# GpSimd takes three of the first expert's weight subtractions, and the routing table's products are spread, in an attention and mixture-of-experts kernel

## The chip, the cores and the metric

The kernel runs on one core of a Trainium2 chip. Its time is the device time of one launch in microseconds, the median of the runs shown; three runs of the kernel before gave 868.94, 869.82 and 870.97 us. A core has five engines with a queue of instructions each: TensorE (PE, matrix products), VectorE (DVE), ScalarE (ACT), GpSimd (POOL) and SyncE (SP, which here issues DMAs). An instruction that needs another engine's result waits at the head of its queue, and all behind it on that engine wait too.

## The reference

Three layers in a row, all in float32:

```python
# 1. clustered attention: 2 batches, 8 heads, 768 rows, 64 columns
mask = q_assign[:, :, :, None] == k_assign[:, :, None, :]        # nearest of 16 centroids
scores = np.where(mask, scale * (q @ k.transpose(0, 1, 3, 2)), -1e9)
x = softmax(scores) @ v                                          # -> 1536 rows of 512

# 2. mixture of 8 experts, the two best of each row (D = 512, F = 1024)
noisy = x @ w_gate + np.log1p(np.exp(x @ w_noise)) * noise
top2_w = softmax over the two largest of noisy
out[mask] += top2_w[mask, k, None] * (np.maximum(x[mask] @ w1[e], 0.0) @ w2[e])

# 3. a second mixture of 8 experts: the best of each row, 384 rows per expert at most
out[i] = gate_w[i] * y[expert_idx[i], pos[i]]
```

The change lies in layer 2, in the passage from attention to the experts.

## The kernel before

**Products in float32.** A float32 operand is split into a high part of a shorter format and a low part, the rest. A product is the sum of three: high by high, high by low, low by high. The names end in `h` and `l`: `xh`, `xl` for rows of x, `wh`, `wl` for weights, `hh`, `hl` for the hidden layer. Splitting a weight takes two instructions per group of 1024 columns: ScalarE copies the raw weights into `wh` (L199), and VectorE subtracts, `wl = raw - wh` (L200). A weight matrix has four such groups; SP fetches them through four `raw` buffers (L187). Matrix n = 0 is the first expert's first weights, n = 1 its second, n = 2 the second expert's first.

**Jobs.** Expert 0's rows are done in two jobs of 256 rows, one per half of the batch: `jobs[0]` (rows of batch 0, known early) and `jobs[1]` (batch 1). Both use n = 0 and 1. A wide job goes over eight blocks f of 128 hidden columns (`wide1`, L1072: 12 products, then `hh` on ScalarE at L1074 and `hl` on VectorE at L1075), and then over tiles of 128 rows (`second`, L1117 to L1119: three products for each f, 24 for a tile), whose sum ScalarE copies to y (L1138) and GpSimd scatters to memory (L1159). For the next job GpSimd gathers rows (`xg`, L1010), TensorE turns them (`tp`, L1051), ScalarE makes `xh` (L1053) and VectorE `xl` (L1054).

**The route of the second half.** Beside `jobs[0]` runs `route1(1)`: which two experts each row of batch 1 goes to and at which place of their lists. It is a generator of small VectorE operations; at its end twelve pairs of one-hots (`one_hot`, L298 `ohp` and L300 `ohv`, four buffers each) are multiplied on TensorE and added up (L422) to a table of 96 columns; the sum (L424) and three more steps give `t1k` (L314), the row numbers by which `jobs[1]` gathers. Then come the counts `cnt1i`, which every engine reads into registers (L1440), and the gates (L444 to L470, stored at L472).

**What sets the order.** The order is written out by the program at build time with a planner's clock. `tick(us, pace)` is called between steps of TensorE's work; it hands us times pace units to the generators that run beside, and each `yield c` costs c units, a plain `yield` 1, and a negative c costs -c microseconds, whatever the pace (L962 to L975). The same `tick` lets at most one split of weights (`wstep`) be put into the order if the planner holds its data for landed (L957). `K0` to `K3` are costs inside `route1`. `wneed0(1)` puts one split of n = 1 into the order; `wneed(1)` all that are left. `settle` (L977) ticks until all generators are done.

The fetches of n = 2 wait for the rows: while `st["rush"]` is set none is issued, `gathers` (L1020) clears it, and the first fetch behind it gets a dependency on the last gather (L188).

Of the kernel before, what the change touches and what calls it, by code (L numbers as in the profile page):

```python
# [8 lines left out]
F32 = mybir.dt.float32  # L9
# [4 lines left out]
OP = mybir.AluOpType  # L14
# [12 lines left out]
def kernel(  # L27
# [17 lines left out]
    nc = tc.nc  # L45
# [19 lines left out]
    NJ1 = E + 2  # L65
    GT = 3
    F0, FP, T0, PA = 1, (2, 4), 1.5, 3.0
    K0, K1, K2, K3 = 10, 3, 1.5, 2
    NY = 4
    V0, V1, V2, V3 = 3, 4, 5, 3  # L70
    L1, L2 = 1, 2
# [104 lines left out]
    def wload(n):  # L176

        src = halves[n].rearrange("p (g c) f -> p g c f", g=4)
        nch = 4 * src.shape[2]
        k = 2 * E + 2 * NSP - 1  # L180
        buf = n % 3 if n < k else 3 if n == k else (n - 1) % 3
        for g in range(4):
            raw = {}

            def fetch(g=g, raw=raw):
                raw[0] = stage.tile([128, 1024], F32, name="raw")
                ins = nc.sync.dma_start(raw[0].rearrange("p (c f) -> p c f", c=nch // 4), src[:, g])  # L187
                if st.get("behind"):  # L188
                    tc.add_manual_dep(ins.ins, st.pop("behind").ins.name, mybir.DependencyInfo(
                        mybir.DependencyClass.Sync, mybir.DependencyReason.DATA), reason="the rows go first")  # L190
                clock["dma"] = max(clock["now"] + 2.0, clock["dma"]) + 1.46
                raw["at"] = clock["dma"] + 0.3
            chunks.append(fetch)
            cs = slice(g * 1024, (g + 1) * 1024)

            def op(cs=cs, raw=raw, g=g):
                wh, wl = WB[buf]
                W[n] = [w.rearrange("p (c f) -> p c f", c=nch) for w in (wh, wl)]
                nc.scalar.activation(wh[:, cs], raw[0], AF.Copy)  # L199
                nc.vector.tensor_tensor(wl[:, cs], raw[0], wh[:, cs].bitcast(F32), op=OP.subtract)  # L200
                clock["out"] -= 1
                wfill()

            def part(half, cs=cs, raw=raw, g=g):
                wh, wl = WB[buf]
                W[n] = [w.rearrange("p (c f) -> p c f", c=nch) for w in (wh, wl)]
                src = raw[0][:, half * 512:(half + 1) * 512]
                o = slice(cs.start + half * 512, cs.start + (half + 1) * 512)
                nc.scalar.activation(wh[:, o], src, AF.Copy)
                nc.gpsimd.tensor_tensor(wl[:, o], src, wh[:, o].bitcast(F32), op=OP.subtract)  # L210
                if half:
                    clock["out"] -= 1
                    wfill()
            if n:
                wops.append((n, raw, op))
            else:
                wops.extend((n, raw, lambda half=half, part=part: part(half)) for half in range(2))

    def wfill():
        while clock["out"] < st.get("ahead", SB) and chunks and not st.get("rush"):  # L220
            clock["out"] += 1
            chunks.pop(0)()
# [114 lines left out]
    def route1(b, psum):  # L337
# [61 lines left out]
        f = yield from split_slots(s2[:, 0:2].rearrange("p a j -> p (a j)"), 2 * J, "sf")  # L399

        if b == 0:
            st["cnt0"] = rt.tile([128, E], F32, name="cnt0")
            nc.vector.tensor_copy(st["cnt0"], tot)
            st["base"] = rt.tile([128, E], F32, name="base")
            nc.vector.tensor_add(st["base"], eoff1, tot)
            nc.vector.memset(st["base"][:, 0:1], float(S))
            nc.vector.memset(st["base"][:, E - 1:], float((E - 1) * T + S))
            yield
            at = rt.tile([128, 2 * J], I32, name="at0")
            nc.vector.scalar_tensor_tensor(at, f[:, 0], float(NC1), f[:, 1], op0=OP.mult, op1=OP.add)  # L410
            yield
            ptasks.append(place0(b, at))
        else:
            ps2 = psum()
            hots = []
            for j in range(J + 1):
                if j < J:
                    hots += [one_hot(f, c * J + j, code1[:, b, j, c:c + 1], NC1) for c in range(2)]
                    yield K2
                for c in range(2 if j else 0):  # L420
                    n = 2 * (j - 1) + c
                    nc.tensor.matmul(ps2[:, :NC1], *hots[n], start=(n == 0), stop=(n == 2 * J - 1))  # L422
            yield K3
            nc.vector.tensor_add(st["tab0"], ps2[:, :NC1], st["tab0"])  # L424
            yield
            st["dst1"], st["tok1"] = yield from finish_table(st["tab0"], "t1", True)
            cnt = rt.tile([128, 2 * NJ1], F32, name="cnt1")
            nc.vector.tensor_copy(cnt[:, 0:1], st["cnt0"][:, 0:1])
            nc.vector.tensor_copy(cnt[:, 1:2], tot[:, 0:1])
            nc.vector.tensor_add(cnt[:, 2:E], tot[:, 1:E - 1], st["cnt0"][:, 1:E - 1])  # L430
            nc.vector.tensor_copy(cnt[:, E:E + 1], st["cnt0"][:, E - 1:])
            nc.vector.tensor_copy(cnt[:, E + 1:NJ1], tot[:, E - 1:])
            yield
            nc.vector.tensor_sub(cnt[:, NJ1:], cnt[:, 0:NJ1], lim1)
            ci = rt.tile([128, NJ1 + 1], I32, name="cnt1i")
            nc.vector.tensor_copy(ci[:, 0:NJ1], cnt[:, 0:NJ1])
            yield
            over = rt.tile([128, 1], F32, name="over1")
            nc.vector.tensor_reduce(over, cnt[:, NJ1:], axis=AX.X, op=OP.max)
            yield  # L440
            nc.vector.tensor_scalar(ci[:, NJ1:], over, 0.0, None, op0=OP.max)
            st["cnt1f"], st["cnt1i"] = cnt, ci
            yield
# [495 lines left out]
    def wneed0(n=0):  # L939
        if wops and wops[0][0] <= n:  # L940
            wstep()
# [304 lines left out]
    def work(job, nxt, hook=None):  # L1246
# [32 lines left out]
        if job.wide:  # L1279
            for f in range(F0 if job is jobs[0] else 0, FC):  # L1280
                job.wide1(f, hh, hl)
                if job is jobs[0] and f % 2 == 0:
                    wneed0(1)
                tick(12 * job.n / 2400, PA if job is jobs[0] else 3.0)
        else:
            rest = job.tile1(0, hh, hl, tick, fill)
# [71 lines left out]
    def pool(ph, name, side="left"):  # L1358
# [5 lines left out]
    jobs = [Job(h=0, loads=([2], [], []), n=N2, col=0, key="tok0", src=x_dram[0:S], tok="tok0", dst="dst0", **dict(com, kind="first")),  # L1364
            Job(h=0, loads=([], [3], []), n=N2, col=R1 // 2, **late)]
# [158 lines left out]

    st["rush"] = True
    spawn(route1(1, mpsum))
    jobs[0].gathered = True
    tick(T0)
# [127 lines left out]
    for n, job in enumerate(every):  # L1656
        work(job, every[n + 1] if n + 1 < len(every) else None, hooks.get(n))
# [35 lines left out]
```

## Time and profile before

| | us |
|---|---|
| median of three runs | 869.82 (868.94 to 870.97) |
| the profiled execution, its own time | 877.53 |
| its span, first to last instruction | 875.8 |
| mean granted TensorE clock | 0.975 of full speed |
| PE busy | 838.8 (96%) |
| DVE busy | 541.9 (62%) |
| ACT busy | 498.1 (57%) |
| POOL busy | 280.9 (32%) |

The profile is of one execution. A time in it is from the start of the span. `x4` behind a row means that several instructions in a row are put together; square brackets give the idle time of the engine ahead of it and what ended it. Attention ends at about 291 us, `jobs[0]` goes on to 323, `jobs[1]` begins at 325. A granted clock of 1.00 is 2.4 GHz of TensorE, 0.50 is 1.2 GHz.

### The profile page before, as it was taken

To read this page: it belongs to the slowest core of one execution; us is meant where nothing else is said; L and a number is where in the kernel's file an instruction comes from. 1 tells how busy PE (TensorE), PEld (TensorE's weight loads), DVE (VectorE), ACT (ScalarE), POOL (GpSimd) and SP (SyncE) were. 2 spreads that over 40 slices of the span, in tenths; PEclk is the share of its full clock that TensorE was granted. 3 is DMA by queue.
4 is the path that set the end of the run, shared out by engine and by line. 5 is a ranking of instruction groups with operands and counts; after the bars stand their busy time and mean duration, and the time that the engine had idled before them with its cause. 6 is when DMAs were issued, how large, how long until landed. Compare 5 with 4: busy or idle time off the path is not lost. (4 is left out here: it accounts for less than half of the span.)

```text
span 875.8 us, 14860 instructions
## 1 busy us (share of the span) xinstructions
PE 838.8 (96%) x5371; PEld 748.1 (85%) x5371; DVE 541.9 (62%) x1110; ACT 498.1 (57%) x967; POOL 280.9 (32%) x465
## 2 busy tenths in 40 slices
PE   8899999999998989999999999999998988999997
PEld 6799999889987878989989898988987767888886
DVE  6888888989888656447444353535477337655270
ACT  5798988888998315445333343535344336555361
POOL 3445556447864021321302122033221112222110
PEclk9799999999999979999999999999899989999999
DMA  4005422411113035744644444458374318866250
GB/s 98 28 28 199 143 96 73 139 32 47 55 37 107 19 126 169 222 153 138 189 162 138 135 145 137 120 186 287 107 257 140 128 51 295 264 204 221 73 171 17
DMA packets 62189, 116.84 MB, mean 133 GB/s; under 512 B 13737, under 2 KB 25769, under 8 KB 62096
## 3 DMA queue, kind: packets, MB, share of 16 engines
q1 hardware_dynamic: 52832, 92.60, 33.1%
q0 software_dynamic: 9264, 23.06, 8.2%
q8 instruction: 51, 0.84, 0.4%
q14 instruction: 42, 0.34, 0.1%
HBM read 97.29 MB, written 23.74 MB: 138 GB/s over the span
## 5 line engine op out<-in xcount | busy, mean ns | idle before, releaser
L200 DVE TENSOR_TENSOR wl<-raw,wh 128x1024 fp32r<-128x1024 f32 x124 | 150.5, 1222 | 40.0 <-ACT wh L199 36.1
L1072 PE MATMUL l<-xh,wh 128*128 128x256 f32 (+1 forms) x508 | 156.4, 310 | 2.7 <-ACT xh L1053 1.2
L1072 PE MATMUL l<-xh,wl 128*128 128x256 f32 (+1 forms) x508 | 155.2, 308 | 0.2 <-DVE wl L200 0.2
L1072 PE MATMUL l<-xl,wh 128*128 128x256 f32 (+1 forms) x508 | 148.1, 307 | 0.0
L1117 PE MATMUL l<-wh,hh 128*128 128x512 f32 x328 | 137.1, 418 | 1.2 <-PEq L1445 0.4
L199 ACT ACTIVATE wh<-raw 128x1024 fp32r<-128x1024 f32 x124 | 128.9, 1053 | 4.9 <-DMA raw<-in_moe_w_dram 4.8
L1119 PE MATMUL l<-wh,hl 128*128 128x512 f32 x328 | 131.0, 399 | 0.0
L1118 PE MATMUL l<-wl,hh 128*128 128x512 f32 x328 | 130.4, 398 | 0.0
L1075 DVE SCALAR_TENSOR_TENSOR hl<-l,hh 128x256 fp32r<-128x256 f32 (+1 forms) x127 | 61.3, 484 | 98.4 <-ACT hh L1074 95.0
L1074 ACT ACTIVATE hh<-l 128x256 fp32r<-128x256 f32 (+1 forms) x127 | 55.1, 434 | 104.5 <-PE l L1072 102.9
L776 DVE TENSOR_TENSOR El<-et,Eh 128x384 fp32r<-128x384 f32 x192 | 101.2, 557 | 12.2 <-ACT Eh L775 10.0
L1072 PEld LDWEIGHTS l<-xh,wh 128*128 128x128 f32 x508 | 96.3, 190 | 6.2 <-issue 2.8
L744 DVE TENSOR_REDUCE nm<-st 128x1 f32<-128x768 f32 x96 | 91.4, 952 | 13.7 <-PE st L739 12.8
L1072 PEld LDWEIGHTS l<-xh,wl 128*128 128x128 f32 x508 | 96.1, 189 | 1.2 <-DVE wl L200 0.4
L775 ACT ACTIVATE Eh<-et 128x384 fp32r<-128x384 f32 x192 | 87.7, 495 | 12.5 <-PE et L770 12.2
L1072 PEld LDWEIGHTS l<-xl,wh 128*128 128x128 f32 x508 | 93.6, 188 | 0.2
L753 ACT ACTIVATE E<-st,nm 128x768 f32<-128x768 f32 x96 | 87.0, 907 | 8.2 <-DVE nm L744 7.9
L1159 POOL DMA_INDIRECT y_dram<-y,t1d x23 | 23.3, 1012 | 194.0 <-ACT y L1138 164.8
L770 PE MATMUL et<-identr,Er 128*128 128x128 f32 x576 | 72.6, 244 | 4.4 <-DVE El L776 2.4
L1119 PEld LDWEIGHTS l<-wh,hl 128*128 128x128 f32 x328 | 62.8, 191 | 15.0 <-DVE hl L1089 0.3
L770 PEld LDWEIGHTS et<-identr,Er 128*128 128x128 f32 x576 | 65.5, 142 | 11.0 <-DVE El L776 3.7
L1117 PEld LDWEIGHTS l<-wh,hh 128*128 128x128 f32 x328 | 62.8, 191 | 13.5 <-issue 1.5
(322 smaller groups left out, 1558.5 us busy)
## 6 DMA issues: line engine op xcount, KB each, us to landing
raw<-in_moe_w_dram SPq DMA_DIRECT2D x128, 512.0 KB, 4.5
vraw<-in_v_dram SPq DMA_DIRECT2D x16, 192.0 KB, 2.5
x_dram<-xp SPq DMA_DIRECT2D x8, 384.0 KB, 3.3
out_dram<-xg SPq DMA_DIRECT2D x1, 3072.0 KB, 10.2
y_dram<-xg SPq DMA_DIRECT2D x1, 3072.0 KB, 10.3
part<-y_dram SPq DMA_DIRECT2D x12, 256.0 KB, 3.7
yt<-y_dram SPq DMA_DIRECT2D x12, 256.0 KB, 3.9
x_dram<-part POOLq DMA_DIRECT2D x12, 256.0 KB, 3.7
```

The costliest lines, as they stand in the source:

```text
L199: nc.scalar.activation(wh[:, cs], raw[0], AF.Copy)
L200: nc.vector.tensor_tensor(wl[:, cs], raw[0], wh[:, cs].bitcast(F32), op=OP.subtract)
L744: nc.vector.tensor_reduce(nm, ps, axis=AX.XY, op=OP.max, negate=True)
L753: made = nc.scalar.activation(E, st.pop(("S", i, j))[:, :, :HW], AF.Exp, bias=st.pop(("nm", i, j)), accum_out=st["Z", i][:, j:j + 1])
L770: ins = nc.tensor.transpose(ps[:, n * 128:(n + 1) * 128].bitcast(F32R), E[:, part, n * 128:(n + 1) * 128], identr)
L775: nc.scalar.activation(Eh[o], ps, AF.Copy)
L776: nc.vector.tensor_sub(El[o], ps, Eh[o].bitcast(F32))
L1072: nc.tensor.matmul(ps[:, :n], (w1l if k == 2 else w1h)[:, c, fs], (self.xl if k == 1 else self.xh)[:, c, :n], start=(m == 0), stop=(m == l ...
L1075: nc.vector.scalar_tensor_tensor(hl[:, f, :n], ps[:, :n], 0.0, hh[:, f, :n].bitcast(F32), op0=OP.max, op1=OP.subtract)
L1117: nc.tensor.matmul(ps[:rows], hh[:, f, cs], w2h[:, f, :], start=(f == 0), stop=False)
L1118: nc.tensor.matmul(ps[:rows], hh[:, f, cs], w2l[:, f, :], start=False, stop=False)
L1119: nc.tensor.matmul(ps[:rows], hl[:, f, cs], w2h[:, f, :], start=False, stop=(f == FC - 1))
```

## The change

Three edits. The low parts of groups 1 to 3 of n = 1 are made on GpSimd in two halves of 512 columns instead of on VectorE in one piece. The four splits of n = 1 stand behind the blocks f = 2, 3, 4 and 6 (before: 2, 4 and 6, and the fourth behind f = 7). And the costs in `route1(1)` are others: K1 is 1 instead of 3; the first pair step costs 1 unit and each later one 0.88 us of the planner's clock, instead of 1.5 units each.

```diff
-    K0, K1, K2, K3 = 10, 3, 1.5, 2
+    K0, K1, K2, K3 = 10, 1, -0.88, 2
...
                 nc.scalar.activation(wh[:, cs], raw[0], AF.Copy)
-                nc.vector.tensor_tensor(wl[:, cs], raw[0], wh[:, cs].bitcast(F32), op=OP.subtract)
+                if n == 1 and g:
+                    for o in range(0, 1024, 512):
+                        at = slice(cs.start + o, cs.start + o + 512)
+                        nc.gpsimd.tensor_tensor(wl[:, at], raw[0][:, o:o + 512], wh[:, at].bitcast(F32), op=OP.subtract)
+                else:
+                    nc.vector.tensor_tensor(wl[:, cs], raw[0], wh[:, cs].bitcast(F32), op=OP.subtract)
                 clock["out"] -= 1
...
                     hots += [one_hot(f, c * J + j, code1[:, b, j, c:c + 1], NC1) for c in range(2)]
-                    yield K2
+                    yield K2 if j else 1
...
-                if job is jobs[0] and f % 2 == 0:
+                if job is jobs[0] and f in (2, 3, 4, 6):
                     wneed0(1)
```

Lines below the new code are numbered 5 higher in the changed kernel. On TensorE the twelve table products stood six behind the sixth group of the first tile and six behind its end; now they stand four behind the sixth group, two behind the tile's end, and two and four behind the second and fourth group of the second tile. On GpSimd six subtractions stand ahead of the scatter of the first tile. Further on the instructions are the same in the same order.

VectorE in the last blocks of `jobs[0]` before, up to the copy of the ranks (`l_4895` is the block f = 4, `l_4949` f = 7):

```order
L1075 SCALAR_TENSOR_TENSOR hl<-l_4895,hh 128x256
L200 TENSOR_TENSOR wl_4796<-raw,wh_4795 128x1024
L265 TENSOR_REDUCE fwm<-fw 128x6
L267 TENSOR_TENSOR oh_4848<-fw,fwm 128x48
L370 TENSOR_TENSOR A_4915<-oh_4848 128x48
L1075 SCALAR_TENSOR_TENSOR hl<-l_4917,hh 128x256
L1075 SCALAR_TENSOR_TENSOR hl<-l_4932,hh 128x256
L200 TENSOR_TENSOR wl_4796<-raw,wh_4795 128x1024
L1075 SCALAR_TENSOR_TENSOR hl<-l_4949,hh 128x256
L200 TENSOR_TENSOR wl_4796<-raw,wh_4795 128x1024
L379 COPY rs<-rps 128x56
```

The same place in the changed kernel (`l_4898` is f = 4, `l_4954` f = 7):

```order
L1080 SCALAR_TENSOR_TENSOR hl<-l_4898,hh 128x256
L270 TENSOR_REDUCE fwm<-fw 128x6
L272 TENSOR_TENSOR oh_4848<-fw,fwm 128x48
L375 TENSOR_TENSOR A_4919<-oh_4848 128x48
L1080 SCALAR_TENSOR_TENSOR hl<-l_4921,hh 128x256
L1080 SCALAR_TENSOR_TENSOR hl<-l_4936,hh 128x256
L1080 SCALAR_TENSOR_TENSOR hl<-l_4954,hh 128x256
L384 COPY rs<-rps 128x56
```

Three subtractions are gone from between the hidden layer's and the route's operations.

ScalarE at the end of `jobs[0]` before, from the copy of the first tile's sum to the first `hh` of `jobs[1]` (`wh_4797` is the matrix n = 2):

```order
L1138 ACTIVATE y<-l_4979 128x512
L447 ACTIVATE gt<-gt 128x6
L1053 ACTIVATE xh<-tp 128x4x128
L1138 ACTIVATE y<-l_5089 128x512
L1053 ACTIVATE xh<-tp 128x4x128
L1440 TENSOR_LOAD cnt1i
L1074 ACTIVATE hh<-l_5316 128x256
```

The same place in the changed kernel:

```order
L1143 ACTIVATE y<-l_4984 128x512
L452 ACTIVATE gt<-gt 128x6
L1143 ACTIVATE y<-l_5077 128x512
L199 ACTIVATE wh_4797<-raw 128x1024
L1445 TENSOR_LOAD cnt1i
L1058 ACTIVATE xh<-tp 128x4x128 x2
L1079 ACTIVATE hh<-l_5321 128x256
```

A copy of the matrix n = 2 and the register load stand ahead of both `xh`, which stood ahead of them.

VectorE at the same time before, from the gates to the first `hl` of `jobs[1]`:

```order
L461 TENSOR_TENSOR gates_105<-gw 128x6
L465 TENSOR_SCALAR gt<-s_5000 128x6
L466 TENSOR_SCALAR gt<-s_5000 128x6
L468 TENSOR_TENSOR gt<-gt 128x6
L470 TENSOR_TENSOR gates_105<-gates_105,gt 128x6x2
L1054 TENSOR_TENSOR xl<-tp,xh 128x4x128 x2
L1440 TENSOR_LOAD cnt1i
L1075 SCALAR_TENSOR_TENSOR hl<-l_5316,hh 128x256
```

And in the changed kernel:

```order
L466 TENSOR_TENSOR gates_105<-gw 128x6
L205 TENSOR_TENSOR wl_4798<-raw,wh_4797 128x1024
L463 TENSOR_TENSOR gw<-gt 128x6
L464 TENSOR_TENSOR gw<-gt,s_4997 128x6
L466 TENSOR_TENSOR gates_105<-gw 128x6
L470 TENSOR_SCALAR gt<-s_4997 128x6
L471 TENSOR_SCALAR gt<-s_4997 128x6
L473 TENSOR_TENSOR gt<-gt 128x6
L475 TENSOR_TENSOR gates_105<-gates_105,gt 128x6x2
L1445 TENSOR_LOAD cnt1i
L1059 TENSOR_TENSOR xl<-tp,xh 128x4x128 x2
L1080 SCALAR_TENSOR_TENSOR hl<-l_5321,hh 128x256
```

A subtraction for n = 2 stands in the middle of the gates, and the register load ahead of `xl`. On SP the four fetches of n = 2 stand ahead of the store of the gates, which stood ahead of them.

## Rows read from the trace of the kernel before

**Rows 1.** TensorE: line L1119 (ns, starts), then timeline (start, us, what, [idle]).

```profile
L1119 PE MATMUL l<-wh,hl x6: 389/396/397, 303.8 to 307.3; 128*128 128x512 f32 x6
...
308.77 2.53 PE L422 MATMUL rps<-ohv,ohp 128*128 128x96 f32 x6 [1.05 <-DVE ohv L300]
...
323.13 1.03 PE L1051 MATMUL tp<-ident,xg 128*128 128x128 f32 x8
325.39 0.38 PE L1072 MATMUL l<-xh,wh 128*128 128x256 f32 x1 [1.23 <-ACT xh L1053]
...
326.44 0.63 PE L1072 MATMUL l<-xl,wh 128*128 128x256 f32 x4
```

**Rows 2.** Windows: length, busy PE, PEld, DVE, ACT, POOL, clock, DMA share, GB/s.

```profile
307.70:311.10 3.40, 2.04 (x7) 1.38 (x7) 3.33 (x17) 0.00 (x0) 0.00 (x0) 0.80 0.00 0
311.10:319.80 8.70, 8.70 (x24) 6.87 (x25) 5.94 (x39) 0.80 (x2) 3.10 (x3) 0.50 0.19 59
```

**Rows 3.** VectorE's timeline, 304 to 326.

```profile
304.59 0.42 DVE L1075 SCALAR_TENSOR_TENSOR hl<-l,hh 128x256 fp32r<-128x256 f32 x1
304.92 1.21 DVE L200 TENSOR_TENSOR wl<-raw,wh 128x1024 fp32r<-128x1024 f32 x1
306.06 0.21 DVE L379 COPY rs<-rps 128x56 f32<-128x56 f32 x1
...
308.10 0.29 DVE L298 TENSOR_SCALAR ohp<-lane,sf 128x128 fp32r<-128x128 bf16 x1
...
308.54 0.28 DVE L298 TENSOR_SCALAR ohp<-lane,sf 128x128 fp32r<-128x128 bf16 x1
...
315.61 0.26 DVE L424 TENSOR_TENSOR tab<-rps,tab 128x96 f32<-128x96 f32 x1 [0.54 <-PE rps L422]
...
316.44 0.21 DVE L314 TENSOR_SCALAR t1k<-t1d 128x96 int32<-128x96 int32 x1
...
318.89 0.16 DVE L458 TENSOR_TENSOR gw<-gt 128x6 f32<-128x6 f32 x1
...
319.71 0.17 DVE L470 TENSOR_TENSOR gates<-gates,gt 128x12 f32<-128x12 f32 x1
...
325.37 0.69 DVE L1054 TENSOR_TENSOR xl<-tp,xh 128x512 fp32r<-128x512 f32 x1 [0.28 <-ACT xh L1053]
```

**Rows 4.** ScalarE's timeline, two rows.

```profile
303.16 0.38 ACT L1074 ACTIVATE hh<-l 128x256 fp32r<-128x256 f32 x1
...
324.74 0.60 ACT L1053 ACTIVATE xh<-tp 128x512 fp32r<-128x512 f32 x1
```

**Rows 5.** GpSimd, L210, the halves of n = 0: ns min/median/max, first and last start.

```profile
L210 POOL TENSOR_TENSOR wl<-raw,wh x8: 1269/1285/1299, 252.0 to 276.7; 128x512 fp32r<-128x512 f32 x8
```

**Rows 6.** Second gather, fetch behind it, SP's waits (us, times, longest), a landing.

```profile
318.25 1.00 POOL L1010 DMA_INDIRECT xg<-x_dram,t1k  x1 [0.30 <-issue]
...
321.67 1.77 SPq L187 DMA_DIRECT2D raw<-in_moe_w_dram  x4
...
SPq L187 <- DVE hl L1075: 10.4, 4, 5.1
SPq L187 <- DMA xg<-x_dram,t1k: 1.4, 1, 1.4
...
raw<-in_moe_w_dram SPq DMA_DIRECT2D x1, 512.0 KB, 3.6
```

**Rows 7.** The register loads, L1440: ns min/median/max, start.

```profile
L1440 ACTq TENSOR_LOAD <-cnt1i x1: 1402/1402/1402, 324.2 to 324.2; - x1
...
L1440 DVEq TENSOR_LOAD <-cnt1i x1: 1555/1555/1555, 325.4 to 325.4; - x1
```

**Rows 8.** Windows at two other places, columns as in rows 2.

```profile
21.30:23.00 1.70, 0.00 (x0) 0.00 (x0) 1.67 (x7) 1.37 (x4) 0.38 (x3) 1.00 0.17 61
23.00:26.40 3.40, 3.35 (x20) 3.04 (x20) 2.59 (x7) 2.61 (x8) 0.24 (x2) 0.50 0.00 0
...
706.30:712.50 6.20, 6.20 (x15) 4.85 (x16) 0.00 (x0) 0.60 (x1) 3.02 (x3) 0.50 0.16 40
```

## The prediction

> **What bounds the kernel now.** I read the windows of the stretch first, then TensorE's, VectorE's and ScalarE's own rows, then the queue of the DMA issues. The change touches only the passage from the first expert's first job to its second one, at 300 to 330 us of the profiled execution; the order of the instructions on all five engines is the same before and behind it. In this passage TensorE is the engine that everything shifts with, and it loses time twice. It waits 1.05 us for the first one-hot [rows 1], because VectorE comes to the one-hots late; then the twelve table products run at the pace at which VectorE makes their operands. In that thin stretch its granted clock falls (0.80 on the mean from 307.70 to 311.10, 0.50 from there to 319.80 [rows 2]), that is from 2.4 to 1.2 GHz, and 8.7 us of matmuls run at half pace, some 4.3 us lost. Behind it the second job starts at 325.39, after a wait of 1.23 us for its operand xh; the products that want xl start at 326.44 without a further wait [rows 1]. This last time is the one to beat: from there on TensorE runs without a gap, so what the change gains or loses is read at the first xl product of the second job.
>
> **The change, part by part.** *Three subtractions leave VectorE.* Each takes 1.21 us and the next instruction starts 1.14 us behind its start [rows 3]. In their place the last hl of the job is due when hh is copied: 303.16 + 0.38 = 303.54 [rows 4], so hl starts at 303.57, the copy of the ranks 0.33 behind it at 303.90 instead of 306.06 [rows 3]: 2.16 us earlier (the earlier copies of the weights on ScalarE fall into its idle time in front of hh, so hh stays where it was). The first one-hot then starts at 305.94 instead of 308.10.
>
> *Six half subtractions on GpSimd* take 1.27 to 1.30 us each by the same operation of this kernel [rows 5]. The three copies they follow end at about 297.6, 299.6 and 303.1, so the pairs end at 300.2, 302.8 and 305.7; the products that read them are the groups for f = 2, 4 and 6 at 303.28 + 0.70 f, that is 304.7, 306.1 and at the earliest 307.5 (a group of three every 0.70 us: the six L1119 products start between 303.8 and 307.3 [rows 1]). The cover is 1.8 us at the least; I cost this edit at nothing, from 0 to the price in rival B.
> The Trainium skill's GPSIMD Engine Reference, section Specifications, says that GpSimd shares its SBUF interfaces with VectorE and contends with VectorE instructions that have two SBUF inputs, which nearly all instructions of the route are. By that rule the halves would be longer than in [rows 5] and the cover could go; the rows show a spread of 30 ns only, so I take them.
>
> *The table products are spread.* A pair of one-hots takes 0.44 us [rows 3] and four buffers hold them, so a fifth waits for the first product. Now four products stand behind the sixth group, two behind the eighth, two and four behind the second and fourth group of the next tile. From 305.94 on, the fourth operand is ready at 307.8; TensorE comes there at 307.55, so it waits 0.2 to 0.4 us and not 1.05. With some 0.1 us for a product (at full clock unseen: the rows have the six of [rows 1] at the pace of their operands; between 0 and 0.4 us each) the four end at 308.0, the next two run at 309.4, the next two at 311.0, their buffers let the last two pairs be made by 312.3, and the last four run from 312.7 to 313.1. The sum into the table follows at 313.15; from its start to the end of t1k is 1.04 us (315.61 to 316.44 + 0.21 [rows 3]), so the row numbers are ready at 314.2 instead of 316.65: 2.45 us earlier. TensorE stays full until the tile's end at about 316, so I expect the full clock there, and the tile ends 7 us earlier than 323.13, where the transposes start now [rows 1].
>
> *What is late next.* The rows of the second job are gathered only when t1k is there. The second gather starts 1.60 us behind t1k (318.25 against 316.65) and has landed 3.4 us after its start, when SP, which waits for it, goes on at 321.67 [rows 6]: 319.2 instead. TensorE, ready at 316, waits for it. The transposes then need xh from ScalarE and xl from VectorE, and here the order of the changed kernel is another one: in both engines a copy of the next weights (buffer n = 2) now stands ahead of xh and of xl, and on VectorE the register load as well. These weights are fetched by SP, and SP holds that fetch until the gather has landed (1.4 us of waiting for xg [rows 6]); the first of the four lands 3.6 us after its issue [rows 6]. So in the changed kernel the first weights land at 319.2 + 3.6 = 322.8, and nothing of xh or xl can start before.
> On ScalarE: copy from 322.8; the register load takes 1.40 us beside it [rows 7]; then xh twice, 0.60 us each, 0.49 apart (the second at 324.74 today [rows 4]): the second ends at 325.4. TensorE starts the second job at 325.4, as today (325.39).
> On VectorE: wl starts behind that copy at 323.9, the rest of the gates' arithmetic 1.14 later at 325.1, its last instruction 0.82 after that (318.89 to 319.71 [rows 3]) at 325.9, then the register load, 1.56 us [rows 7], to 327.5, then two xl of 0.69 us [rows 3]: 328.9. Nothing hides this load: today it comes behind both xl and starts when the second of them does (325.37), so I let it wait for the instruction ahead of it here too. The first xl product starts at 328.95 instead of 326.44: 2.5 us late.
> The Trainium skill's Advanced Engine Details and Errata, section Engine Queue Depths, gives VectorE and ScalarE a queue of 8 instructions. By that the register load could run while wl is still at work, and the delay would be that of rival C; the trace gives no sign of it, since VectorE's load starts at 325.4 with the xl ahead of it [rows 7].
>
> *The clock.* TensorE now idles from 316 to 319.2, from 320.3 to 325.4 and from 326.4 to 328.9. After 1.7 us without a matmul (21.30 to 23.00) the trace shows the clock at 0.50, and it stayed there through the next 3.4 us of full work in one place and 6.2 us in another [rows 8]. Half of that is lost: 1.7 to 3.1 us; I take the middle, 2.3 (after so long a gap that the fall itself is certain).
>
> *Smaller moves.* The store of the gates stands behind the four weight fetches on SP and waits for the late gates; the fetches behind it waited for hl of the second job, 10.4 us in all [rows 6], so they have room. The scatter of the last tile goes out some 7 us earlier and may share the DMA engines with the first weights: 0 to 0.6 us on their landing.
>
> The sum: 2.5 + 2.3 = 4.8 us slower. The profiled execution took 877.53 us (span 875.8 and 1.7 around it), 7.7 above the median of 869.82; the shift lies in one passage, so I carry it over in microseconds: 877.53 becomes 882.3, and the median **874.6**. With the ends of the unknown terms (clock 1.7 to 3.1 or not at all, landing 0 to 0.6 later) the likeliest case reaches from 872.3 to 876.1.
>
> **The rivals.** *A: faster.* The mechanism is that the copy of the weights doesn't hold xh and xl: its fetch is let go earlier than the gather, or lands beside the transposes. Then xh follows the transposes as today (325.39 - 323.13 = 2.26 us from their start to the first product), the job starts at 319.2 + 2.3 = 321.5, its xl at 322.6, 3.8 us earlier than 326.44; the idle 3.2 us in front may still cost 1.7 of clock: 866.0 to 867.7. It decides if the weights land before about 320. For it: VectorE is 2.2 us ahead and the low clock goes. Against it: the wait of SP for xg stands in the rows, and the order of ScalarE. Chance 0.13.
> *B: slower by more.* GpSimd's halves take twice as long beside VectorE, 2.6 us: pairs end at 302.8, 307.9 and 313.1, the group f = 6 waits from 309.8 to 313.1, the table and all behind it come 5 us later: some 10 us slower, 879.8. It decides from about 1.6 us a half. Against it: [rows 5]. Chance 0.06.
> *C: no change.* The register load runs beside wl, so the two xl follow the gates' last instruction (325.9 + 0.17) and end at 327.4, 1.0 us late, and the clock is up again at once: 870.8. Something later that waits today could also take up the shift. For it: the load's place in the queue is unseen in this form; against it: TensorE's long gaps. Chance 0.09.
> *D: the change doesn't spread the products in time.* The fourth operand comes late and TensorE thins out again, with the clock down before 316. That costs little itself, since TensorE waits at 316 anyway, but puts t1k back by up to 1 us: 875.6, inside the forecast's range. It belongs to the forecast's 0.72.
>
> **How the numbers follow.** Forecast 0.72 at 874.6, A 0.13, B 0.06, C 0.09. A later low-clock stretch that falls otherwise can move any case by 1 to 2 us (such stretches last 3.4 to 6.2 us at half pace [rows 8]), so I widen 872.3 to 876.1 to 870.3 to 877.6; that leaves out A, B and little else. What this kernel can tell from no change is about 0.2%, 1.7 us: 868.1 to 871.6. Faster 0.13, same 0.10 (C and the lower edge of the forecast), slower 0.77.
>
> **What would show it.** Right: the copy of the one-hots' chain 2.2 us earlier, full clock from 303 to 316, table products that wait under 0.5 us; the second gather at about 315.8; ScalarE waiting for raw until about 322.8 with xh behind it; VectorE idle from about 317 to 324, and TensorE waiting for xl until about 329, at half clock for some microseconds after. Wrong: if xh follows the transposes within a microsecond, if the first xl product starts before 326.4, or if the clock is 1.00 from 329 on, the forecast's sum falls with it.

## The result: 1.3% slower, twice what was forecast

The changed kernel takes 880.92 us in the median of four runs (880.47 to 886.09), the kernel before 870.39 in four runs (868.94 to 872.34). The ratio of the means is 1.0133, with a 95% interval from 1.009 to 1.0176: about 10.5 us more, where 4.8 were forecast, and outside the range given. A second series, beside other runs of the kernel before, gave 1.0103 (1.0067 to 1.014).

| | before | changed |
|---|---|---|
| median of the runs, us | 870.39 | 880.92 |
| profiled execution, us (span) | 877.53 (875.8) | 880.87 (878.9) |
| TensorE busy in the span, us | 838.8 | 831.5 |
| waits of TensorE, 294 to 345 us | 3.1 | 13.5 |

The two profiled spans differ by 3.1 us only, because the one of before lost time in other places: its attention ended 2.86 us later, with a granted clock of 0.50 from 23.00 to 26.40 and from 33.20 to 40.00 (changed: from 22.20 to 29.00 alone), and from 613.50 to 620.00 it ran TensorE at 0.50 where the changed one had 1.00. So I count from one instruction that the change doesn't touch, GpSimd's last addition to the gate's logits LG (start at 293.09 before, 290.23 changed), to the first scatter of the second job's sums (`y_dram` by `t1d`). Columns here and in all timelines below: start, duration, engine, line, what, and in brackets the idle time before it and who ended it.

```profile
293.09 0.39 POOL L821 TENSOR_TENSOR LG<-LG,lt 128x96 f32<-128x96 f32 x1 [9.38 <-DVE lt L819]
346.25 1.41 POOL L1159 DMA_INDIRECT y_dram<-y,t1d  x1 [14.12 <-ACT y L1138]
```

And the same two rows of the changed kernel:

```profile
290.23 0.39 POOL L826 TENSOR_TENSOR LG<-LG,lt 128x96 f32<-128x96 f32 x1 [9.36 <-DVE lt L824]
353.75 1.41 POOL L1164 DMA_INDIRECT y_dram<-y,t1d  x1 [27.20 <-ACT y L1143]
```

That is 53.16 us before and 63.52 changed: 10.36 us are lost in this passage, about the whole of the measured difference. It stays lost: at the last of these scatters, some 240 us later, the difference is 10.71 us (290.28 before, 300.99 changed; the first row is of before, the second of the changed kernel).

```profile
583.37 0.88 POOL L1159 DMA_INDIRECT y_dram<-y,t1d  x1 [3.38 <-DVE y L1154]
591.22 0.88 POOL L1164 DMA_INDIRECT y_dram<-y,t1d  x1 [3.38 <-DVE y L1159]
```

Three marks divide the passage:

| from ... to | before | changed | difference | forecast |
|---|---|---|---|---|
| LG, to the end of t1k | 23.56 | 26.66 | +3.10 | -2.45 |
| to the first xl product of the second job | 9.79 | 14.97 | +5.18 | +4.96 |
| to the first scatter of the second job | 19.81 | 21.89 | +2.08 | +2.3 |
| sum | 53.16 | 63.52 | +10.36 | +4.8 |

Two of the three terms came out as forecast. The first has the wrong sign.

### The profile page after: what moved, and what is told of

Its sections match the earlier page's. It is cut to its first block, busy times and chain, and to the rows that moved or that the text cites. A ratio compares the mean times of both kernels' runs of the same rounds, so it can differ in the third digit from the quotient of the medians.

```text
span 878.9 us, 14868 instructions
## 1 busy us (share of the span) xinstructions
PE 831.5 (95%) x5371; PEld 743.3 (85%) x5371; DVE 541.9 (62%) x1107; ACT 498.4 (57%) x967; POOL 288.4 (33%) x471
## 5 line engine op out<-in xcount | busy, mean ns | idle before, releaser
L205 DVE TENSOR_TENSOR wl<-raw,wh 128x1024 fp32r<-128x1024 f32 x121 | 146.8, 1222 | 46.3 <-ACT wh L199 42.3
L1077 PE MATMUL l<-xh,wh 128*128 128x256 f32 (+1 forms) x508 | 158.9, 315 | 10.2 <-ACT xh L1058 5.9
L1077 PE MATMUL l<-xh,wl 128*128 128x256 f32 (+1 forms) x508 | 157.4, 312 | 0.2 <-DVE wl L205 0.2
L1077 PE MATMUL l<-xl,wh 128*128 128x256 f32 (+1 forms) x508 | 150.7, 312 | 1.4 <-DVE xl L1059 1.4
L1077 PEld LDWEIGHTS l<-xh,wh 128*128 128x128 f32 x508 | 98.4, 194 | 13.6 <-ACT xh L1058 6.1
L1077 PEld LDWEIGHTS l<-xh,wl 128*128 128x128 f32 x508 | 98.1, 193 | 1.2 <-DVE wl L205 0.4
L1077 PEld LDWEIGHTS l<-xl,wh 128*128 128x128 f32 x508 | 95.8, 193 | 1.8 <-DVE xl L1059 1.6
```

The lines of the kernel that those rows point to most:

```text
L1077: nc.tensor.matmul(ps[:, :n], (w1l if k == 2 else w1h)[:, c, fs], (self.xl if k == 1 else self.xh)[:, c, :n], start=(m == 0), stop=(m == l ...
```

## The profile after

*The first term, up to t1k.* VectorE beside GpSimd's halves in the changed kernel:

```profile
294.72 1.22 DVE L205 TENSOR_TENSOR wl<-raw,wh 128x1024 fp32r<-128x1024 f32 x1
295.86 1.30 DVE L265 TENSOR_TENSOR fw<-nl,f1m 128x48 f32<-128x48 f32 x1
297.19 1.18 DVE L267 TENSOR_TENSOR fw<-fw,first 128x48 f32<-128x48 f32 x1
298.41 0.20 DVE L270 TENSOR_REDUCE fwm<-fw 128x6 f32<-128x48 f32 x1
298.64 0.95 DVE L272 TENSOR_TENSOR oh<-fw,fwm 128x48 f32<-128x48 f32 x1
299.52 0.41 DVE L1080 SCALAR_TENSOR_TENSOR hl<-l,hh 128x256 fp32r<-128x256 f32 x1
299.85 0.97 DVE L371 SCALAR_TENSOR_TENSOR nl<-oh,nl 128x48 f32<-128x48 f32 x1
```

Five of GpSimd's six halves in the same stretch, one by one (timeline; then the line's group: ns min/median/max, first and last start), to be read against [rows 5]:

```profile
294.75 2.33 POOL L203 TENSOR_TENSOR wl<-raw,wh 128x512 fp32r<-128x512 f32 x1 [4.13 <-ACT wh L199]
297.05 1.25 POOL L203 TENSOR_TENSOR wl<-raw,wh 128x512 fp32r<-128x512 f32 x1
298.27 1.25 POOL L203 TENSOR_TENSOR wl<-raw,wh 128x512 fp32r<-128x512 f32 x1
299.49 1.27 POOL L203 TENSOR_TENSOR wl<-raw,wh 128x512 fp32r<-128x512 f32 x1
...
305.59 1.29 POOL L203 TENSOR_TENSOR wl<-raw,wh 128x512 fp32r<-128x512 f32 x1
...
L203 POOL TENSOR_TENSOR wl<-raw,wh x6: 1255/1273/2332, 294.8 to 305.6; 128x512 fp32r<-128x512 f32 x6
```

The four rows of 0.95 to 1.30 us are operations on 48 columns that take 0.20 to 0.21 us where GpSimd does nothing. All four read two operands from SBUF, and each ends 0.06 to 0.08 us behind the half that runs beside it: at 297.16, 298.37, 299.59 and 300.82, with halves that end at 297.08, 298.30, 299.52 and 300.76. So it is each time the end of the half that lets them go. The reduction with one operand (0.20) and hl, whose one operand lies in PSUM (0.41), kept their time among them. GpSimd's median is about the old one, 1.27 us; only one half took 2.33, the one that starts 0.03 us behind VectorE's subtraction of 1.22 us. One more operation of VectorE is held later, beside the last half (0.45 us instead of 0.21):

```profile
306.51 0.45 DVE L390 TENSOR_TENSOR rkb<-rs,base 128x48 f32<-128x48 f32 x1
```

Behind the held operations hl comes late, and TensorE with it. The row of the stall, the start of the second layer, and the same two places of before:

```profile
299.98 0.58 PE L1077 MATMUL l<-xh,wh 128*128 128x256 f32 x1 [3.19 <-DVE hl L1080]
...
305.67 0.48 PE L1122 MATMUL l<-wh,hh 128*128 128x512 f32 x1
```

```profile
300.03 0.38 PE L1072 MATMUL l<-xh,wh 128*128 128x256 f32 x1 [0.38 <-DVE hl L1075]
...
303.28 0.48 PE L1117 MATMUL l<-wh,hh 128*128 128x512 f32 x1
```

The clock of TensorE in three stretches (columns as in [rows 2]):

```profile
298.70:305.70 7.00, 5.72 (x37) 5.63 (x37) 4.36 (x12) 1.52 (x3) 3.40 (x4) 0.51 0.00 0
305.70:315.50 9.80, 9.75 (x52) 8.02 (x49) 7.87 (x36) 0.79 (x2) 2.24 (x2) 1.00 0.07 27
322.70:336.10 13.40, 6.31 (x28) 6.02 (x29) 4.97 (x13) 3.89 (x7) 2.94 (x4) 0.50 0.65 230
```

The stall of 3.19 us, less the 0.38 of before, makes 2.81 us. Behind it TensorE runs at 1.2 GHz (0.51 in the first stretch) and needs 5.69 us to the second layer instead of 3.25: 2.44 more. With the 0.24 us of the operation held beside the last half that is 5.49, nearly the whole of the 5.55 us by which t1k missed its forecast (-2.45 to +3.10). In the place of the low clock of [rows 2] there is now the full one, as forecast, and the table products hardly wait:

```profile
309.95 0.79 PE L427 MATMUL rps<-ohv,ohp 128*128 128x96 f32 x4
312.03 0.32 PE L427 MATMUL rps<-ohv,ohp 128*128 128x96 f32 x2
```

*The second term, from t1k to xl.* ScalarE, VectorE's three late rows, and TensorE, against [rows 1, 3 and 4]:

```profile
325.81 1.06 ACT L199 ACTIVATE wh<-raw 128x1024 fp32r<-128x1024 f32 x1 [6.51 <-DMA raw<-in_moe_w_dram]
327.30 1.08 ACT L1058 ACTIVATE xh<-tp 128x512 fp32r<-128x512 f32 x2 [0.43 <-issue]
```

```profile
326.90 1.23 DVE L205 TENSOR_TENSOR wl<-raw,wh 128x1024 fp32r<-128x1024 f32 x1 [7.68 <-ACT wh L199]
...
328.86 0.17 DVE L475 TENSOR_TENSOR gates<-gates,gt 128x12 f32<-128x12 f32 x1
330.52 1.29 DVE L1059 TENSOR_TENSOR xl<-tp,xh 128x512 fp32r<-128x512 f32 x2 [1.49 <-issue]
```

```profile
320.58 0.66 PE L1056 MATMUL tp<-ident,xg 128*128 128x128 f32 x4 [1.92 <-DMA xg<-x_dram,t1k]
...
328.44 0.58 PE L1077 MATMUL l<-xh,wh 128*128 128x256 f32 x1 [5.85 <-ACT xh L1058]
331.86 1.22 PE L1077 MATMUL l<-xl,wh 128*128 128x256 f32 x4 [1.35 <-DVE xl L1059]
```

The turned rows lie ready at 322.6, and xh waits till 327.3 behind a copy of weights that the second job doesn't need: ScalarE waits 6.51 us for that copy's data. On VectorE the register load takes its full time between the gates and xl: the 1.49 us of issue.

## The experiments

In each the mark is the first scatter of the second job, counted from the LG addition; between the two profiled executions of the changed kernel it differed by 0.01 us (63.52 and 63.51). The passage is read from one profiled execution of each kernel. Each ratio is against runs of the kernel before beside it on the same chip, and these differed by chip: 876.49 us in the median beside e1 to e4, 877.33 beside e5 to e7, 871.67 beside e8 and the second series of the changed kernel. The times that the expectations of e1 to e4 name were missed: 886.30, 876.93, 879.43 and 886.08 us were measured. Less the 6.10 us by which before was slower there than in the first series, e2 to e4 fall inside, and e1 is 1.2 us above.

| kernel | t1k | to xl product | to scatter | sum | ratio of the runs, interval |
|---|---|---|---|---|---|
| before | 23.56 | 9.79 | 19.81 | 53.16 | 1 |
| changed | 26.66 | 14.97 | 21.89 | 63.52 | 1.0133 (1.009 to 1.0176) |
| changed, again | 26.67 | 14.87 | 21.97 | 63.51 | 1.0103 (1.0067 to 1.014) |
| e1, subtractions on VectorE | 23.36 | 14.78 | 21.66 | 59.80 | 1.0109 (1.0073 to 1.0145) |
| e2, only GpSimd's subtractions | 23.14 | 7.71 | 20.45 | 51.30 | 0.9998 (0.9971 to 1.0025) |
| e3, xh and xl put ahead | 25.77 | 8.43 | 21.57 | 55.77 | 1.0049 (1.0025 to 1.0073) |
| e4, in quarters | 23.85 | 15.02 | 21.85 | 60.72 | 1.0118 (1.0081 to 1.0154) |
| e5, e1 and e3 | 23.38 | 8.42 | 21.32 | 53.12 | 1.0021 (0.9989 to 1.0052) |
| e6, deferred on VectorE | 20.17 | 9.03 | 22.56 | 51.76 | 1.0001 (0.9974 to 1.0027) |
| e7, one operand | 22.15 | 14.74 | 21.63 | 58.52 | one run, 882.03 us |
| e8, e6 with the gates later | 20.15 | 9.47 | 20.53 | 50.15 | 0.9963 (0.9927 to 0.9998) |

The shift of each sum against 53.16, in us, lies inside the interval of its ratio (e1: +6.64 in 6.4 to 12.7; e8: -3.01 in -6.4 to -0.2), though for e1 and e4 near its lower end, so the passage explains the runs as finely as they can tell. The runs alone speak for the price of the order (e3's 1.0049 is below both series of the changed kernel), but not for that of GpSimd's subtractions: e1 (1.0109) can't be told from the changed kernel (1.0103 and 1.0133). That one is read from the passage.

**The subtractions back on VectorE** (e1_vector).

```diff
-                if n == 1 and g:
+                if n == 1 and g > 9:
```

> The changed kernel with its three subtractions put back on VectorE (the new places of the copies and the new spacing of the table products stay). Theory L (a GpSimd subtraction holds up VectorE operations that read two operands from SBUF, and a copy of the next weights then stands ahead of xh and xl in the queues): VectorE's small route operations take 0.2 us again instead of 0.95 to 1.30, TensorE waits about 0.4 us and not 3.2 for the hl of block f = 3, and the clock is 1.00 there; but xh and xl still wait for the raw weights, so from the end of t1k to the first xl product it is again 14 to 15 us. Time 875 to 879, above before and below the changed kernel's 881. Rival Q (the queue order alone costs the 10 us, GpSimd costs nothing): as slow as the changed kernel or slower, 881 to 884, since VectorE has 3.6 us more to do.

VectorE's operations were back at 0.20 and 0.21 us, the wait for hl at 0.38, and the clock stayed up until 318:

```profile
295.94 0.20 DVE L265 TENSOR_TENSOR fw<-nl,f1m 128x48 f32<-128x48 f32 x1
296.17 0.21 DVE L267 TENSOR_TENSOR fw<-fw,first 128x48 f32<-128x48 f32 x1
...
298.70:318.00 19.30, 16.31 (x90) 12.63 (x89) 14.59 (x67) 3.12 (x6) 4.11 (x4) 1.00 0.12 36
```

t1k came 3.30 us earlier than in the changed kernel. The second term stayed (14.78), and with it most of the loss.

**Only GpSimd's subtractions** (e2_pool_only): the kernel before with the loop of the change that subtracts on GpSimd, and nothing else of it.

> The kernel before with one edit: the three subtractions on GpSimd in halves (places of the copies, spacing of the table products and the order of xh and xl as before). Theory L: VectorE's operations with two SBUF operands that fall beside a GpSimd half (1.27 us) take 0.9 to 1.3 us instead of 0.2; what VectorE saves (3.4 us) is spent on these waits, t1k comes at the same time or up to 2 us later, time 870 to 875. Rival Q (GpSimd costs nothing): t1k 2.2 us earlier, operations 0.2 us, time 866 to 869.

No difference in the runs, and t1k only 0.42 us earlier (23.14): three subtractions of 1.21 us left VectorE, and five operations of VectorE between 300.53 and 307.95 took 0.85 to 1.27 us instead of 0.15 to 0.21. That is nearer to theory L (t1k the same or later) than to rival Q (2.2 us earlier). With xh and xl still ahead of the weights, the second job's first xl product was 2.50 us early (30.85 against 33.35). In the runs it isn't seen.

**xh and xl put ahead** (e3_order): in the changed kernel the copies xh and subtractions xl of the second job stand ahead of the register loads and of the copies of n = 2.

```diff
         if hook:
+            if job is jobs[0]:
+                fill()
+                while todo:
+                    fill()
             hook()
...
+        held.add(2)
         settle()
+        held.discard(2)
```

> The changed kernel with xh, xl and the transposes put ahead of the register loads and of the first copy of the next weights (GpSimd subtractions and spacing stay). Theory L: the stall of VectorE at the front stays (operations of 0.95 to 1.30 us, TensorE waiting 3.2 us for hl), but xh follows the transposes within 1 us, from the end of t1k to the first xl product it is 8.5 us and not 15, time 872 to 876. Rival Q: the whole loss is gone, 866 to 870. Rival G (GpSimd costs all of it, the queue order nothing): 880 to 882.

The stretch from t1k to the xl product fell from 14.97 to 8.43 us, and the ratio from 1.0133 and 1.0103 to 1.0049. What was left is the hold-up at the front, unchanged (3.19 us for hl) but with a shorter low clock behind it (0.50 from 301.90 to 305.30; t1k 0.89 us earlier than in the changed kernel), and a clock that fell behind the transposes (0.50 from 322.50 to 329.10):

```profile
300.63 0.39 PE L1077 MATMUL l<-xh,wh 128*128 128x256 f32 x1 [3.19 <-DVE hl L1080]
...
323.23 0.55 PE L1077 MATMUL l<-xh,wh 128*128 128x256 f32 x1 [0.92 <-ACT xh L1058]
```

**GpSimd in quarters** (e4_quarters): twelve instructions of 256 columns instead of six of 512.

> The changed kernel with the GpSimd subtractions in twelve quarters of 256 columns instead of six halves of 512. Theory L, if a VectorE operation with two SBUF operands waits until the GpSimd instruction that runs has ended: the four held operations take 0.5 to 0.7 us instead of 0.95 to 1.30, TensorE waits 1.2 to 2 us for hl instead of 3.2, time 876 to 880. If the hold-up goes by GpSimd's whole work and not by its instructions: as the changed kernel, 881. Rival Q: 881 too, with operations of the same length as in halves.

A quarter took 0.735 us in the median, and VectorE's held operations came down with it:

```profile
298.97 0.75 DVE L265 TENSOR_TENSOR fw<-nl,f1m 128x48 f32<-128x48 f32 x1
299.76 0.65 DVE L267 TENSOR_TENSOR fw<-fw,first 128x48 f32<-128x48 f32 x1
300.44 0.20 DVE L270 TENSOR_REDUCE fwm<-fw 128x6 f32<-128x48 f32 x1
300.68 0.41 DVE L272 TENSOR_TENSOR oh<-fw,fwm 128x48 f32<-128x48 f32 x1
```

TensorE waited 1.58 us for hl instead of 3.19, the clock stayed at 1.00 (301.50 to 308.50), and t1k came 2.81 us earlier than in the changed kernel. The runs can't show that (1.0118).

**Both hold-ups away** (e5_vector_order): e1 and e3 together.

> The changed kernel with the subtractions back on VectorE and, beside that, the copies xh and the subtractions xl of the next job put ahead of the register loads and ahead of the next weights' copies. The theory: what the change loses is two things, VectorE's small operations held while GpSimd subtracts (some 5.5 us) and xh and xl standing behind weight copies and register loads (some 5 us from the table to the first xl product). With both taken away, only the spread table products stay. Then VectorE's operations of the slot search are back at 0.20 to 0.21 us, the table's end to the first xl product falls from 14.97 to 8 to 9 us, that product stands 31.5 to 32.5 us behind GpSimd's last add (before 33.35, changed 41.63), and the time is 0.997 to 1.003 of the kernel before; a low-clock stretch where TensorE waits may take away what the 1 us gives. The rival: the spread table products themselves cost, because they let TensorE fall idle or make the one-hots late; then the ratio stays at 1.004 or more, as with GpSimd's subtractions and the new order (1.0049), though both hold-ups are gone.

Sum 53.12 against 53.16, ratio 1.0021 with 1 inside its interval. The xl product came 1.55 us early, and a clock of 0.55 from 319.00 to 326.00 gave it back (19.81 became 21.32). So what stays of the change in this kernel, the spread of the table products and the new places of the copies, neither costs nor brings anything together with e3's order, and the loss is made of the other two. Four kernels show their sizes by the sum: GpSimd's subtractions cost 3.72 with the late xh and xl (63.52 - 59.80) and 2.65 without (55.77 - 53.12), the order of xh and xl 7.75 (63.52 - 55.77) or 6.68 (59.80 - 53.12). Each pair differs by 1.07 us, of which 0.89 is e3's earlier t1k, behind the shorter low clock.

**One operand** (e7_one_operand).

```diff
-    nc.gpsimd.tensor_tensor(wl[:, at], raw[0][:, o:o + 512], wh[:, at].bitcast(F32), op=OP.subtract)
+    nc.gpsimd.tensor_scalar(wl[:, at], wh[:, at].bitcast(F32), 1.0, 1.0, op0=OP.mult, op1=OP.mult)
```

> The changed kernel with another instruction of the same shape in the place of GpSimd's subtraction: the high part times one, a single operand in SBUF, written to the same place. The low parts of the weight groups 1 to 3 then hold the high parts, so the values of the first expert's second layer are not the reference's; everything else stands as in the changed kernel. Theory one: it is GpSimd's instruction with two operands in SBUF that holds VectorE's instructions with two operands in SBUF; with one operand VectorE's operations beside it take 0.20 to 0.21 us again, and TensorE's wait for hl falls from 3.19 to about 0.4 us. Theory two: any elementwise instruction of GpSimd over SBUF holds them for its length; then the VectorE operations that stand beside a GpSimd half take 0.5 to 1.3 us as in the changed kernel (0.95 to 1.30), by the length of a half.

GpSimd's instruction was shorter itself, 0.613 us in the median (and 1.71 for the one that starts beside VectorE's 1.22 us subtraction). VectorE's operations beside it were still held, and took up to that length:

```profile
295.46 1.22 DVE L205 TENSOR_TENSOR wl<-raw,wh 128x1024 fp32r<-128x1024 f32 x1
296.59 0.62 DVE L265 TENSOR_TENSOR fw<-nl,f1m 128x48 f32<-128x48 f32 x1
297.24 0.56 DVE L267 TENSOR_TENSOR fw<-fw,first 128x48 f32<-128x48 f32 x1
297.84 0.20 DVE L270 TENSOR_REDUCE fwm<-fw 128x6 f32<-128x48 f32 x1
298.07 0.31 DVE L272 TENSOR_TENSOR oh<-fw,fwm 128x48 f32<-128x48 f32 x1
```

Theory one falls: an operand less doesn't free VectorE. The longest held operation goes with the length of GpSimd's instruction: 1.30 us by 1.27, 0.75 by 0.735 (e4), 0.62 by 0.613.

**Deferred on VectorE** (e6_defer): the aim of the change met without GpSimd, from the kernel before. One deferred subtraction stands at f == 6, two behind t1k; `K1` and `K2` are 0.1 and -0.93, and the edits of e3 are in it too.

```diff
+                if n == 1 and g:
+                    st.setdefault("lows", []).append(low)
...
+                for f in range(FC):
+                    nc.tensor.matmul(ps[t], hh[:, f, cs], w2h[:, f, :], start=(f == 0), stop=False)
+                    nc.tensor.matmul(ps[t], hl[:, f, cs], w2h[:, f, :], start=False, stop=False)
+                    if f % 2 == 1:
+                        tick(0.93)
...
+            for f in range(FC):
+                for t, rows in self.main:
+                    nc.tensor.matmul(ps[t], hh[:, f, self.cols(t, rows)], w2l[:, f, :], start=False, stop=(f == FC - 1))
```

> The kernel before with the aim of the change met without GpSimd: the subtractions of groups 2 and 3 stand on VectorE behind the table (group 1's at the last block of the first layer), the second layer's products with the high weights come first, with the table products spread between them, the products with the low weights last, and xh and xl go ahead of the register loads. The theory: nothing on VectorE is held by GpSimd (operations of the slot search 0.20 to 0.21 us), 2.4 us of subtractions leave the path to the table, and the 16 products with low weights (about 0.22 us each, 3.5 us) cover the flight of the gathered rows instead of standing ahead of the table. Then the first xl product of the next job stands 27.5 to 30 us behind GpSimd's last add (before 33.35) and the ratio is 0.993 to 0.998. The rival, after the kernel with only the GpSimd edit, which had that product 2.5 us earlier and was no faster (0.9998): what comes behind this place is bounded by something else (the transfers of the next weights, or the clock); then the product is just as early and the ratio is 0.998 to 1.002.

t1k came 3.39 us earlier than before and the xl product 4.15, with no low clock (1.00 from 294.00 to 345.00). But 2.75 us were given back by the scatter: TensorE waited twice for hl, which stood behind the gates, the register load and subtractions of the next weights on VectorE. The rival was right on the time (1.0001); whether the transfers or the order on VectorE made it so is what e8 asks:

```profile
332.54 0.38 PE L1080 MATMUL l<-xh,wh 128*128 128x256 f32 x1 [1.33 <-DVE hl L1083]
334.86 0.39 PE L1080 MATMUL l<-xh,wh 128*128 128x256 f32 x1 [0.64 <-DVE hl L1083]
```

**The gates later** (e8_gates): e6 with one statement changed.

```diff
-        settle()
+        while "cnt1i" not in st:
+            tick(0.3)
```

> The kernel with the deferred subtractions once more, with one thing moved: the gates' operations and the first copies and subtractions of the next weights no longer stand ahead of the next job's first blocks on VectorE, but between its hl. With the deferred subtractions the first xl product was 4.15 us earlier than before, counted from GpSimd's last add, and the first scatter of the next job only 1.4 us (51.76 against 53.16): TensorE waited there twice for hl (1.33 and 0.64 us) behind weight subtractions. The theory: those waits go, the scatter stands 48.5 to 50.5 us behind the add, and the ratio is 0.994 to 0.998. The rival: the next weights' transfers decide there (the copies waited 1.45 and 0.76 us for them), the scatter stays at 51 to 52 us and the ratio at 0.998 to 1.002.

Both waits for hl are gone, and the sum is 50.15, inside the forecast, so it was the order: with the next weights' operations between the hl, their transfers hold nothing up. The ratio is 0.9963 (0.9927 to 0.9998): 867.69 against 871.67 us, a version faster than both kernels, if by little more than the runs can tell. TensorE has no further wait in the second job's first layer after this one:

```profile
317.79 0.55 PE L1080 MATMUL l<-xh,wh 128*128 128x256 f32 x1 [1.25 <-ACT xh L1061]
```

**The changed kernel again** (e9_changed_again), on one chip with e8.

> The changed kernel as it is, once more, so that it stands on the same chip and beside the same runs of the kernel before as others do. First theory (two hold-ups, of about 7 us for xh and xl behind weight copies and register loads and 2.5 to 4 us for GpSimd's subtractions, the spread products nothing): the ratio is 1.010 to 1.014, and the first scatter of the next job stands 62 to 65 us behind GpSimd's last add (before 53.16, first profile 63.52). The rival: part of the 10.5 us first measured was the state of the clock in few runs; then the ratio is 1.004 to 1.009.

Sum 63.51 and ratio 1.0103: the loss doesn't hang on the first few runs. The held operations are there again (1.29, 1.19, 0.95, 0.97 us).

## Why the prediction was wrong

*Six half subtractions on GpSimd: this step failed.* It was costed at nothing, because the halves have 1.8 us of cover and their length stands in [rows 5]. Both held: five of the six halves kept 1.25 to 1.29 us, and no product waited for one. I had asked only what VectorE does to GpSimd, and not the reverse. The price is paid on VectorE, where an operation with two SBUF operands is held until the half beside it ends. It came to 5.49 us at t1k: 2.81 of stall, 2.44 of low clock behind it and 0.24 beside the last half. e1 shows it by taking the halves away: the same operations take 0.20 us, t1k is 3.30 us earlier, though VectorE has its subtractions back. [rows 5] list GpSimd's side alone; the trace of before shows VectorE's too, in the attention, where the same lines run for the first half of the batch beside other GpSimd instructions, and it was overlooked:

```profile
180.27 1.02 POOL L617 TENSOR_TENSOR qt<-qraw,qt 128x384 fp32r<-128x384 f32 x1
180.40 0.96 DVE L262 TENSOR_TENSOR fw<-fw,first 128x48 f32<-128x48 f32 x1
...
203.58 0.51 POOL L706 TENSOR_TENSOR cwt<-cs,cmx 128x192 f32<-128x192 f32 x1 [1.04 <-DVE cmx L700]
203.69 0.44 DVE L291 CAST sf<-si 128x24 f32<-128x24 int32 x1
```

With GpSimd idle the same two lines take 0.21 us (at 298.95) and 0.18 (at 307.89). From these rows a price for VectorE could have been carried. The Trainium skill's GPSIMD Engine Reference, section Specifications, which the prediction weighed and put aside, names this contention, and the trace agrees, with 0.95 to 1.30 us in the place of 0.20. The Trainium skill's SBUF — State Buffer, section SBUF: two separate sides, is plainer: the shared pair of ports is an exclusive lock, whoever starts first has it for the whole instruction. The hold that goes with GpSimd's length in the changed kernel, e4 and e7, and the one half of 2.33 us beside VectorE's 1.22 agree with that in both directions.

*Three subtractions leave VectorE.* The step is right by itself. Where they are put off without GpSimd (e6), the ranks are copied 10.89 us behind the LG addition (304.95 and 294.06) instead of 12.97 (306.06 and 293.09): 2.08 us earlier, 2.16 forecast. With the subtractions on GpSimd (e2, 306.04 and 293.73) it is 0.66. The further gain of e6 at t1k (3.39 us) comes with its other edits; no run parts them.

*The table products are spread.* They were, with waits under 0.4 us and the full clock from 305.70 to 315.50; but the clock fell earlier instead, after the stall for hl, which the forecast of a full clock from 303 on didn't see. Up to t1k it is worth little with the subtractions on VectorE: e5 has it, and t1k at 23.38 against 23.56. Rival D's thin stretch didn't come.

*What is late next.* Right in mechanism and size: 14.97 us from t1k to the xl product, 14.75 forecast; the copy of the first weights 8.92 us behind t1k, 8.6 forecast; the second gather 1.59 us behind the end of t1k; the register load a full 1.49 us between the gates and xl. Rival C's load beside wl didn't occur. e3 shows it is the order: 8.43 us with xh and xl ahead.

*The clock behind it.* Right: 2.08 us to the first scatter against 2.3, with 0.50 granted from 322.70 to 336.10.

*Rival B* had its time (879.8) near the measured one by luck, and its mechanism wrong: the halves did not take longer, and TensorE waited for hl and not for their result. Rival A's early weights did not come.

*From the profiled execution to the median.* The forecast carried a shift over in microseconds. That held: 10.36 us in the passage, 10.5 in the medians.

## What to carry to other kernels

That GpSimd is idle and its results come in time doesn't make work on it free: look which VectorE instructions with two SBUF operands run beside it, and count each as held until the GpSimd instruction ends. The trace of the kernel before may have the price already: look for a VectorE instruction that takes longer than its like and ends with a GpSimd instruction. Shorter GpSimd instructions helped here (quarters: t1k 2.81 us earlier), and so did another moment on VectorE: the ranks came 2.08 us earlier in e6, 0.66 with the same subtractions on GpSimd (e2). And when a hint moves one kind of work forward in an in-order queue, look which wait it brings along: a copy that waits 6.5 us for its data held the two operations that TensorE needed next.

## What was not expected of the hardware

- A GpSimd instruction over SBUF holds VectorE's operations with two SBUF operands, with one operand of its own as with two: operations of 0.20 us took up to 1.30, 0.75 and 0.62 us beside instructions of 1.27, 0.735 and 0.613 us, and in the changed kernel each ended 0.06 to 0.08 us behind the GpSimd instruction. A reduction with one operand (0.20 us) and an operation with an operand in PSUM (0.41) went on beside them. Reading one operand only doesn't always free a VectorE operation: in the trace of before a cast took 0.44 us instead of 0.18 and ended with GpSimd's instruction (204.13 and 204.09).
- It works the other way too: the GpSimd half that starts beside VectorE's 1.22 us subtraction took 2.33 us instead of 1.27, and in e7 1.71 instead of 0.613.
- A stall of 3.19 us at the front cost nearly as much again by the clock: 2.44 us, with products at 1.2 GHz behind it. In e3 the low clock behind the same stall was shorter (0.50 from 301.90 to 305.30), and e4, with a stall of 1.58 us, kept the full clock.

Still open: e6's sum is 1.4 us below that of before and its runs are level with it, inside an interval of 2.3 us either way. Nothing in the rest of the layer takes the gain back: at the last scatter (583.01) e6 is still 1.33 us ahead, and e8 (577.48, LG addition at 290.02) 2.82. Whether the low-clock stretches behind it, which fall differently in each execution, take it, these runs can't tell.
